# One decode step of attention and a gated MLP on one core: the query weights loaded in eight parts instead of one

## The chip, the cores and the metric

The kernel runs on one core of a Trainium2 chip. The metric is the device time of one execution in microseconds (us). Three executions of the kernel before took 2521.19, 2520.79 and 2520.80 us, median 2520.80 us.

## What is computed

One token `x` (1 x 512, bf16) goes through an attention block with a cache of 32 heads of 65,536 positions of 128 numbers, and through a gated MLP. A sigmoid gate mixes the two results.

```python
def _A_ref(x, k_cache, v_cache, wq, wo):          # wq: 512 x 4096, wo: 4096 x 512
    q = (x @ wq).reshape(B, Sq, H, Dh).transpose(0, 2, 1, 3)      # H = 32, Dh = 128
    scores = jnp.einsum("bhqd,bhkd->bhqk", q, k_cache) * (Dh ** -0.5)
    p = softmax(scores, axis=-1)
    o = jnp.einsum("bhqk,bhkd->bhqd", p, v_cache)
    return o.transpose(0, 2, 1, 3).reshape(B, Sq, H * Dh) @ wo

def _B_ref(x, w_gate, w_up, w_down):              # 512 x 1792, 512 x 1792, 1792 x 512
    return (silu(x @ w_gate) * (x @ w_up)) @ w_down

g = sigmoid((x * gate_w).sum(-1, keepdims=True))
out = g * A + (1 - g) * B
```

The keys and the values are 537 MB each. Every byte of them is needed once.

## The kernel before, in words

One large array in on-chip memory, `mem`, has 128 partitions with 184 slots of 512 bf16 numbers each. All weights and all parts of the cache are loaded into slots of it. SyncE issues nearly all loads from one queue, in the order in which its block is written (lines 201 to 244).

**The start.** `weights` (lines 207 to 209) issues one load of one weight array and lets it raise that array's semaphore by 16. Line 211 loads `wq` into the slots from `V0` on: 128 rows, one for each partition, of 16,384 bf16 numbers (32 KB), which makes 4,096 KB. Partition p gets rows 4p to 4p + 3 of `wq`, which lie one after the other in HBM. Lines 212 to 214 load `wg`, `wu` and `wd` in the same way (1,792 KB each), and line 217 the first half of head 0's keys in two loads of 4,096 KB. None of these seven issues waits for anything. Then SyncE waits for `s_q` (line 219) before it issues the second half of head 0's keys, because these go to the slots that `wq` has taken.

**The queries.** TensorE waits at line 436 until the semaphore of `wq` shows 16, makes all 32 heads' queries in 128 matmuls (line 439) and signals `s_q` (line 441). VectorE and TensorE bring the queries into the form that the scores need (lines 371 to 376 and 445). After that TensorE waits for `wg` and `wu` (line 467 holds the matmuls) and for `wd` (line 475).

**The heads.** For each head, VectorE transposes the keys in 16 pieces (line 331 for head 0, lines 399 and 406 for the others), and TensorE multiplies each piece by the query (line 455). A softmax follows (lines 272, 299, 301, 274), and VectorE rearranges its result (line 340). While the next head's scores are made, TensorE adds up the values (line 502). A cache half is one load of 8,192 KB. SyncE issues it (line 205) when the slots that it goes to have been read, which it learns from `ktdone` (keys transposed) or `pvdone` (values used).

**The end.** The values of the second part of the last head and `wo` arrive in smaller pieces (lines 235 to 244), the last products are made (lines 516, 531, 549), and ScalarE sends the result out (line 310).

Of the kernel before, what the change touches and what calls it, by code (L numbers as in the profile page):

```python
# [5 lines left out]
P = 128  # L6
KB = 512
# [13 lines left out]
def bass_gated_mix__mha_block_cached__swiglu_ffn__decode_kernel(  # L21
# [11 lines left out]
    out: bass.AP,  # L33
):
    _, H, S, Dh = A_k_cache.shape
    D = A_wq.shape[0]
    F = B_w_gate.shape[1]
    Dc = D // P
# [24 lines left out]
    with ExitStack() as ctx:  # L63
        def sb(name, shape, dt):
            return ctx.enter_context(nc.sbuf_tensor(name, shape, dt))
# [4 lines left out]
        def sem(name):  # L70
            return ctx.enter_context(nc.semaphore(name))
# [10 lines left out]
        mem = sb("mem", [P, MEM * KB], BF16)  # L82
# [24 lines left out]
        def at(kb, n):  # L107
            return mem[:, kb * KB:kb * KB + n]
# [9 lines left out]
        d = {n: sem("d_" + n) for n in names}  # L118
# [55 lines left out]
        w_dram = {  # L174
            "wq": A_wq.rearrange("(p c) n -> p (c n)", c=Dc),
            "wg": B_w_gate.rearrange("(p c) f -> p (c f)", c=Dc),
            "wu": B_w_up.rearrange("(p c) f -> p (c f)", c=Dc),
            "wd": B_w_down.rearrange("(p c) n -> p (c n)", c=FC),
            "wo": A_wo.rearrange("(p j) n -> p (j n)", p=P),
        }  # L180
        w31_dram = A_wo.rearrange("(h d) n -> h d n", d=Dh)[H - 1]
        WQ, WG, WU, WD, WO = V0, 0, 14, V0 + 64, 64
# [8 lines left out]
        def place(kind, h, z):  # L191
            if kind == "k":
                return (KA, V0)[z] if h == 0 else (KA, KZ)[z]
            return (VA, VZ)[z]

        def kv_dram(cache, h):
            return cache[0, h].rearrange("(b p r) d -> b p (r d)", b=2, p=P)
# [3 lines left out]
        @block.sync  # L201
        def _(sp):
            def load(kind, h, z):
                cache = A_k_cache if kind == "k" else A_v_cache
                sp.dma_start(at(place(kind, h, z), HR * Dh), kv_dram(cache, h)[z]).then_inc(d[kind + "az"[z]], 16)

            def weights(n, kb):
                src = w_dram[n]
                sp.dma_start(at(kb, src.shape[1]), src).then_inc(d[n], 16)  # L209

            weights("wq", WQ)
            weights("wg", WG)
            weights("wu", WU)
            weights("wd", WD)
            half = HR // 2 * Dh
            for n in range(2):
                sp.dma_start(at(KA + 32 * n, half), kv_dram(A_k_cache, 0)[0][:, n * half:n * half + half]).then_inc(  # L217
                    (d["ka0"], d["ka"])[n], 16)
            sp.wait_ge(s_q, 1)
            load("k", 0, 1)  # L220
            for h in range(1, H):
                sp.wait_ge(ktdone, 2 * NP * h - 3 if h > 1 else NP)
                load("k", h, 0)
                if h == 1:
                    sp.wait_ge(ktdone, 2 * NP - 3)
                    sp.wait_ge(s_b, 1)
                else:
                    sp.wait_ge(pvdone, 4 * h - 1)
                load("v", h - 1, 0)
                sp.wait_ge(ktdone, 2 * NP * h + NP // 2)  # L230
                load("k", h, 1)
                sp.wait_ge(pvdone, 4 * h + 1)
                load("v", h - 1, 1)
            sp.wait_ge(ktdone, 2 * NP * H - NP)
            weights("wo", WO)
            src = A_v_cache[0, H - 1].rearrange("(b p r) d -> b p (r d)", b=2, p=P)
            need = {0: (ktdone, 2 * NP * H - 3), 1: (ktdone, 2 * NP * H), 2: (pvdone, 4 * H - 1)}
            for n, (kb, r0, nr) in enumerate(tail):
                if n in need:
                    sp.wait_ge(*need[n])  # L240
                b, o = divmod(r0, HR)
                sp.dma_start(at(kb, nr * Dh), src[b][:, o * Dh:(o + nr) * Dh]).then_inc(dt_[n], 16)  # L242
            sp.wait_ge(pvdone, 4 * H)
            sp.dma_start(at(WO31, D), w31_dram).then_inc(d["w31"], 16)
# [183 lines left out]
        def _(pe):  # L428
# [4 lines left out]
                last = nc.tensor.matmul(psM[:, c:c + 1], xv[:, c, :], ones[0:1, 0:1], start=True, stop=True)  # L433
            last.then_inc(s_xT, 1)
            pe.wait_ge(s_xTb, 1)
            pe.wait_ge(d["wq"], 16)
            for h in range(H):
                for c in range(Dc):
                    last = nc.tensor.matmul(psM[:, 128 + h:129 + h], wq_ap[:, c, h * Dh:(h + 1) * Dh],  # L439
# [47 lines left out]
            with nc.tensor.Fori(0, H) as i:  # L487
                n = i * (2 * NP)
# [90 lines left out]
```

## Time and profile before

| what | value |
|---|---|
| median of three executions | 2520.80 us |
| the profiled execution: its time | 2521.39 us |
| the profiled execution: span, first to last instruction | 2519.6 us |
| time outside the span | 1.8 us |
| read from HBM | 1087.77 MB, 432 GB/s over the span |
| mean granted clock of TensorE | 0.711 of full speed |
| `wq`: issue, and first matmul that uses it | 0.72 us, 13.62 us |

The profile is a page of sums over the span and a trace that can be asked for more. The page has the busy time of each engine, the span in 40 slices, the DMA queues, the chain of work that ended last, and the groups of instructions by line. The trace also has a record of each DMA packet: when it started, how long it took and how many bytes it moved. PE is TensorE, PEld its weight loads, DVE VectorE, ACT ScalarE, POOL GpSimd, and SPq is SyncE's queue. L439 is line 439. A time is counted from the start of the span unless it is a duration.

### The profile page before, as it was taken

To read this page: it belongs to the slowest core of one execution; us is meant where nothing else is said; L and a number is where in the kernel's file an instruction comes from. 1 tells how busy PE (TensorE), PEld (TensorE's weight loads), DVE (VectorE), ACT (ScalarE), POOL (GpSimd) and SP (SyncE) were. 2 spreads that over 40 slices of the span, in tenths; PEclk is the share of its full clock that TensorE was granted. 3 is DMA by queue.
4 is the path that set the end of the run, shared out by engine and by line. 5 is a ranking of instruction groups with operands and counts; after the bars stand their busy time and mean duration, and the time that the engine had idled before them with its cause. 6 is when DMAs were issued, how large, how long until landed. Compare 5 with 4: busy or idle time off the path is not lost.

```text
span 2519.6 us, 46355 instructions
## 1 busy us (share of the span) xinstructions
PE 1587.1 (63%) x21429; PEld 890.1 (35%) x21429; DVE 1397.7 (55%) x1629; ACT 65.6 (3%) x195; POOL 26.9 (1%) x83
## 2 busy tenths in 40 slices
PE   4556756667666576565675665765657656567667
PEld 3333333333333333333333333333333333333334
DVE  3764564554655645646446555466464564654652
ACT  0000000000000000000000000000000000000000
POOL 0000000000000000000000000000000000000000
PEclk8667767677676676676776766767667767677676
DMA  9999999999999999999999999999999999999999
GB/s 419 434 433 432 433 433 434 434 433 433 434 433 433 433 433 433 433 434 434 433 433 433 434 434 436 435 435 433 433 433 433 434 434 434 434 433 433 434 433 386
DMA packets 20332, 1088.00 MB, mean 432 GB/s; under 512 B 2266, under 2 KB 2396, under 8 KB 2780
## 3 DMA queue, kind: packets, MB, share of 16 engines
q1 hardware_dynamic: 20304, 1087.78, 99.9%
q8 instruction: 11, 0.18, 0.0%
q14 instruction: 5, 0.04, 0.0%
q10 hardware_dynamic: 12, 0.00, 0.0%
HBM read 1087.77 MB, written 0.00 MB: 432 GB/s over the span
## 4 chain that ended last, share of the span: by engine, by line
DMA 73%; DVE 14%; issue 11%; PE 1%; SPq 0%; DVEq 0%; ACT 0%
DMA mem<-in_A_k_cache_dram 71%; DVE kt L406 7%; DVE kt L399 6%; DMA mem<-in_A_v_cache_dram 2%; PE psO L502 1%; DVE kt L331 0%; DVE pb L340 0%; DVEq L404 0%; SPq L242 0%; SPq L209 0%; DVEq L397 0%; PE psS L455 0%; PE psZ L549 0%; SPq L217 0%; PE psW L516 0%
## 5 line engine op out<-in xcount | busy, mean ns | idle before, releaser
L455 PE MATMUL psS<-qcur,kt 128*128 128x4 bf16 x16384 | 516.4, 167 | 886.1 <-DVE kt L399 553.2
L502 PE MATMUL psO<-mem,pb 128*4 128x512 bf16 x3968 | 999.6, 417 | 17.0 <-DMA mem<-in_A_v_cache_dram 17.0
L399 DVE STREAM_TRANSPOSE kt<-mem 128x2048 uint32<-128x2048 uint32 x248 | 551.2, 2280 | 578.4 <-DMA mem<-in_A_k_cache_dram 577.4
L455 PEld LDWEIGHTS psS<-qcur,kt 128*128 128x128 bf16 x16384 | 473.8, 104 | 955.1 <-DVE kt L399 586.4
L406 DVE STREAM_TRANSPOSE kt<-mem 128x2048 uint32<-128x2048 uint32 x248 | 547.6, 2275 | 407.5 <-DMA mem<-in_A_k_cache_dram 407.5
L502 PEld LDWEIGHTS psO<-mem,pb 128*4 128x4 bf16 x3968 | 354.4, 91 | 618.7 <-issue 186.2
L340 DVE COPY pb<-pa 32x64 bf16<-32x64 bf16 x1024 | 233.7, 228 | 25.5 <-PE psO L502 10.7
L331 DVE STREAM_TRANSPOSE kt<-mem 128x2048 uint32<-128x2048 uint32 x16 | 35.4, 2278 | 17.0 <-DMA mem<-in_A_k_cache_dram 17.0
L345 DVE TENSOR_REDUCE sm<-psS 128x1 f32<-128x512 f32 x32 | 22.1, 691 | 35.5 <-PE psS L455 35.5
L295 ACT ACTIVATE oTn<-psT,gcol 128x1 bf16<-128x1 f32 x31 | 8.2, 263 | 1113.3 <-PE psT L482 1113.3
L272 POOL PARTITION_ALL_REDUCE sm<-sm x32 | 11.2, 351 | 2392.8 <-DVE sm L345 2392.8
L482 PEld LDWEIGHTS psT<-unit,orow 4*128 4x128 f32 x256 | 30.8, 186 | 14.9 <-issue 13.5
L482 PE MATMUL psT<-unit,orow 4*128 4x1 f32 x256 | 33.5, 248 | 0.8 <-ACT orow L293 0.8
L293 ACT ACTIVATE orow<-psO,sm 4x512 f32<-4x512 f32 x31 | 21.0, 677 | 446.0 <-issue 446.0
L299 ACT ACTIVATE sm<-sm 128x1 f32<-128x1 f32 x32 | 6.5, 203 | 831.0 <-POOL sm L272 831.0
L301 ACT ACTIVATE pa<-psS,sm 128x512 bf16<-128x512 f32 x32 | 22.0, 687 | 1.0
L516 PE MATMUL psW<-pb,mem 128*128 128x1 bf16 x512 | 14.4, 165 | 5.6 <-DMA mem<-in_A_v_cache_dram 4.4
L516 PEld LDWEIGHTS psW<-pb,mem 128*128 128x128 bf16 x512 | 14.0, 102 | 6.8 <-issue 5.1
L274 POOL PARTITION_ALL_REDUCE sm<-sm x32 | 12.3, 384 | 36.4 <-ACT pa L301 36.4
L439 PE MATMUL psM<-xTb,mem 128*128 128x1 bf16 x128 | 3.5, 165 | 11.2 <-DMA mem<-in_A_wq_dram 11.2
L467 PE MATMUL psM<-xTb,mem 128*128 128x1 bf16 x112 | 6.9, 198 | 5.2 <-DMA mem<-in_B_w_up_dram 5.2
L531 PE MATMUL psY<-mem,oR 128*1 128x512 bf16 x32 | 9.7, 477 | 0.3 <-DVE oR L420 0.3
(62 smaller groups left out, 57.8 us busy)
## 6 DMA issues: line engine op xcount, KB each, us to landing
mem<-in_A_v_cache_dram SPq DMA_DIRECT2D x3, 4096.0 KB, 28.5
mem<-in_A_k_cache_dram SPq DMA_DIRECT2D x2, 4096.0 KB, 39.2
mem<-in_A_wq_dram SPq DMA_DIRECT2D x1, 4096.0 KB, 12.8
mem<-in_A_wo_dram SPq DMA_DIRECT2D x1, 4096.0 KB, 34.5
mem<-in_A_v_cache_dram SPq DMA_DIRECT2D x1, 2048.0 KB, 33.0
mem<-in_B_w_gate_dram SPq DMA_DIRECT2D x1, 1792.0 KB, 16.6
mem<-in_B_w_up_dram SPq DMA_DIRECT2D x1, 1792.0 KB, 21.7
mem<-in_B_w_down_dram SPq DMA_DIRECT2D x1, 1792.0 KB, 25.5
```

Source lines behind the costliest of these rows:

```text
L274: nc.gpsimd.partition_all_reduce(Lt, rsum, P, RADD).then_inc(s_L, 1)
L293: nc.scalar.mul(orow[0:4, :], psO[0:4, :], Li[0:4, :]).then_inc(s_or, 1)
L301: nc.scalar.activation(pa[:], psS[:], ACT.Exp, bias=nbias, scale=SCALE, accum_out=rsum).then_inc(expdone, 1)
L331: nc.vector.transpose(kt[:, i % 2, :].rearrange("p (j r t) -> p r j t", j=2, t=32), src.rearrange("p (r j t) -> p r j t", j=2, t=32)).then ...
L340: last = nc.vector.tensor_copy(dst, sr)
L345: nc.vector.reduce_max(mxs, psS[:], AX_X).then_inc(s_mx, 1)
L399: nc.vector.transpose(kt[:, c % 2, :].rearrange("p (j r t) -> p r j t", j=2, t=32), src.rearrange("p (r j t) -> p r j t", j=2, t=32)).then ...
L406: nc.vector.transpose(kt[:, c % 2, :].rearrange("p (j r t) -> p r j t", j=2, t=32), src.rearrange("p (r j t) -> p r j t", j=2, t=32)).then ...
L455: last = nc.tensor.matmul(psS[:, col + 4 * r:col + 4 * r + 4], ktb[c % 2][:, je // 2, r, :, je % 2], qcur[:, je, :], start=(je == 0), stop ...
L482: last = nc.tensor.matmul(psT[:, 0:1], orow[0:4, i * Dh:(i + 1) * Dh], unit[0:4, i:i + 1], start=(i == 0), stop=(i == 3))
L502: last = nc.tensor.matmul(psO[0:4, :], pb[:, 256 * z + r:256 * z + r + 4], vt[:, r * Dh:(r + 4) * Dh], start=(z == 0 and part == 0 and m = ...
L516: last = nc.tensor.matmul(psW[:, 0:1], vt[:, r * Dh:(r + 1) * Dh], pb[:, col:col + 1], start=(col == 0), stop=(col == R - 1))
```

## The change

The load of `wq` becomes eight loads. Load r takes partitions r, r + 8, r + 16 and so on up to r + 120, which are 16 partitions, and the 16 rows of 32 KB in HBM that belong to them. All eight raise the same semaphore, each by 16, and TensorE waits for 128 in place of 16. What lands in which place of `mem` is the same as before.

```diff
-            weights("wq", WQ)
+            for r in range(8):
+                sp.dma_start(mem[r:P:8, WQ * KB:WQ * KB + Dc * H * Dh],
+                             w_dram["wq"].rearrange("(g r) n -> r g n", r=8)[r]).then_inc(d["wq"], 16)
             weights("wg", WG)
...
             pe.wait_ge(s_xTb, 1)
-            pe.wait_ge(d["wq"], 16)
+            pe.wait_ge(d["wq"], 128)
```

## The prediction

> **What bounds the kernel now.** I read the page's top first, for the engines and the data moved.
>
> ```profile
> span 2519.6 us, 46355 instructions
> ...
> DMA  9999999999999999999999999999999999999999
> GB/s 419 434 433 432 433 433 434 434 433 433 434 433 433 433 433 433 433 434 434 433 433 433 434 434 436 435 435 433 433 433 433 434 434 434 434 433 433 434 433 386
> DMA packets 20332, 1088.00 MB, mean 432 GB/s; under 512 B 2266, under 2 KB 2396, under 8 KB 2780
> ## 3 DMA queue, kind: packets, MB, share of 16 engines
> q1 hardware_dynamic: 20304, 1087.78, 99.9%
> ```
>
> All 40 slices show the 16 DMA engines at 90% or more, and 38 of them move 432 to 436 GB/s. SyncE's queue q1 keeps the engines busy 99.9% of the span. No compute engine is above 63%. So the kernel is one stream of bytes, and its time is the stream's length plus a start and a tail.
>
> The packet records give the pace. A row of 32 KB takes an engine 1.213 us in the median and one of 64 KB 2.422 us, and the next row starts at most 0.03 us after the one before has ended. That is 27.0 GB/s for one engine, 432 for 16. The page's load groups sum to 141 loads on q1, and 20304 / 141 = 144 packets: 128 rows and 16 packets of 4 bytes that raise the semaphore, one for each engine. So each engine gets 8 rows of every load.
>
> Does the stream have room in which a delay would vanish? Page part 6 and the waits of SyncE's queue answer that.
>
> ```profile
> mem<-in_A_k_cache_dram SPq DMA_DIRECT2D x63, 29.7
> mem<-in_A_v_cache_dram SPq DMA_DIRECT2D x62, 26.1
> ```
>
> A cache half is 8.39 MB, which takes 19.4 us at 433 GB/s. From issue to landing it takes 29.7 us (keys) and 26.1 us (values). So when a load is issued there are still 10.3 or 6.7 us of other loads ahead of it. SyncE waits long for TensorE (1312.2 us in all) to free the slots, but the engines never run out. What delays the stream at the start is therefore not made up later.
>
> Last, the chain of waits and the timeline of SyncE's queue at both ends.
>
> ```profile
> 0.72 0.38 SPq L209 DMA_DIRECT2D mem<-in_A_wq_dram  x1
> 1.16 0.42 SPq L209 DMA_DIRECT2D mem<-in_B_w_gate_dram  x1
> 1.63 0.45 SPq L209 DMA_DIRECT2D mem<-in_B_w_up_dram  x1
> 2.12 0.53 SPq L209 DMA_DIRECT2D mem<-in_B_w_down_dram  x1
> 2.69 1.04 SPq L217 DMA_DIRECT2D mem<-in_A_k_cache_dram  x2
> 17.20 0.33 SPq L205 DMA_DIRECT2D mem<-in_A_k_cache_dram  x1
> ```
>
> ```profile
> 2480.15 36.12 DMA mem<-in_A_v_cache_dram
> 2516.27 0.05 issue
> 2516.32 0.39 PE psW L516 x8
> ```
>
> Columns are start and duration. The last loads land at 2516.3, and 3.3 us of work follow. At the start, SyncE has issued 18.1 MB by 3.7 us, 42 us of stream. The windows of 0.1 us show the first bytes at 1.7 us, 1.0 us after the issue of `wq`.
>
> **The change, part by part.**
>
> *Seven more issues on SyncE.* From row to row the issues stand 0.44, 0.47, 0.49 and 0.57 us apart, so seven add 2.6 to 4.0 us, some 3.4. `wg`, `wu`, `wd` and the first keys are issued that much later; the last of these at about 6.6 instead of 3.2 us. `wq`'s own bytes (8 x 1.213 = 9.7 us) cover that until 11.4 us. Each of the eight loads brings every engine 1.2 us of work and costs 0.5 us to issue, so the queue grows from the start. Cost: nothing. Were an issue to take over 1.2 us, the stream would have gaps.
>
> *The first bytes.* A shorter first load could start sooner, by at most the 1.0 us between issue and first packet, or not at all. The trace has no load of 16 rows; the nearest row is `wq`'s own. I take nothing.
>
> *Seven more sets of semaphore packets.* Each engine gets 7 more packets of 9 ns (their record): 0.06 us. Rounded, 0.1.
>
> *The wait for 128 in place of 16.* It passes when the last of the eight loads has landed; nothing else is queued on TensorE that could run in between, and VectorE and SyncE wait for `s_q` either way. When `wq` lands is uncritical: the slots of `wq` are wanted at line 219, issued at 17.2 us, while the bytes ahead of it last until 1.7 + 42 = 44 us. That is 26 us of cover. The next stop, `wu` at 23.5 us and the keys at 37.4 us, follows the stream itself.
>
> *Where the rows go.* This is the term that decides. In the load of 128 partitions each engine has eight partitions to itself. In a load of every eighth partition each engine has one row. The trace cannot say whether 27.0 GB/s is the pace of an engine or of the place that it writes to. If partitions are written through 16 groups of eight, each at that pace, and the partitions r, r + 8, ... fall on only half of the groups, then two engines share each group and each goes at half its pace. Order within the load doesn't matter: the 16 partitions are the same. Loads 0 to 3 would use one half of the groups and 4 to 7 the other, always with two engines in each. From below the price is nothing (groups and engines don't meet). From above it is `wq`'s stream once more: 8 x 1.213 = 9.7 us. I take 9.7, since all packet rows of one size show one and the same pace (1.213 to 1.225 us for 90% of the 32 KB rows), which looks like a fixed door rather than shared memory bandwidth, and a door that is full with one engine has nothing left for a second.
>
> [...]
>
> *HBM's side.* The eight loads read rows 256 KB apart (8 x 32 KB). The cache halves have 64 KB rows, so engines four rows apart read 256 KB apart too, at 433 GB/s. Cost: nothing.
>
> **Sum.** The stream after `wq` shifts by 9.7 + 0.1 = 9.8 us, and the end with it. On the profiled execution, 2521.39 (span 2519.6 and 1.8 around it), that is 2531.2. It lies 0.6 above the median 2520.8, so the forecast is 2530.6 us, +0.39%.
>
> **The rivals.**
>
> *A, not slower: a group takes two engines at full pace,* or rows are dealt so that engines don't meet. For it: an engine's own limit explains the constant packets as well. Against it: the fixed pace named above. Time: 2520.8 + 0.1 = 2520.9, at best 2519.9 with an earlier first byte. It decides if a pair reaches together over 1.32 times one engine's pace: 19.4 / 1.32 - 9.7 = 5.0 us, the 0.2% that a measurement can tell from no change.
>
> *B, the two of a pair drift apart.* If one engine of a pair is served first, it finishes its rows of loads 0 to 3 at full pace and moves to the other groups while its partner has the first to itself: 4 + 4 + 4 row times in place of 16. The loss is 4 x 1.213 = 4.9 us: 2525.7. For it: engines do drift, the semaphore packets of `wq` spread over 1.05 us. Against: that spread is less than one row.
>
> *C, each load pays a start.* An engine's first packet stands about 1.88 us before its second (in the earliest record) where later ones are 1.21 apart, 0.66 more. Seven times that is 4.6 us: 2525.5. Against it: in the trace the first packet of `wg` starts 6 ns after the first semaphore packet of `wq`; loads in the queue follow without a gap.
>
> That the change doesn't do what it says is no rival: it is eight plain loads.
>
> **How the numbers follow.** Forecast 0.66 (own range 2528.5 to 2532.5), A 0.17, B 0.10, C 0.05, something dearer 0.02. The predicted time is the forecast's. The range takes in the price's lower bound, nothing, and goes up to what two engines losing another fifth to each other would give, 2532.5: 2520.8 to 2532.5. Half of A lies about its low end. Faster by over 0.2% (below 2515.8) would need more than the 1.7 us that stand before the first byte: 0.01. Within 0.2%: A with C and half of B, less that: 0.17 + 0.05 + 0.05 - 0.01 = 0.26. Slower: 0.73.
>
> **What the changed profile would show.** Right: from 3 to 13 us some 216 GB/s where before had 402; rows of `wq` at some 2.4 us; line 439 starting at 23.4 in place of 13.6 us; the load of line 219 issued at 27 us; the page's first slice at (63 x 419 - 9.7 x 433) / 63 = 352 GB/s, the other 39 as before; q1 with 20304 - 144 + 8 x 32 = 20416 packets; the tail's 3.3 us unchanged. Wrong: line 439 near 13.6 us (A), near 18.5 (B, C), or a first slice of 419. If `wq` lands late and the end doesn't move, the stream had room that I read as none.

## The result, and the profile after

The changed kernel takes 2531.4 us (median of 6 executions, 2531.27 to 2531.56) against 2520.8 us before (6 executions, 2520.66 to 2521.19). The ratio is 1.0041, with a 95% interval of 1.0031 to 1.0051. It is 10.6 us slower; 9.8 us were forecast. The profiled execution took 2531.47 us with a span of 2529.6 us, 10.0 us more than the span before.

The page of the changed kernel, the same rows as before:

```profile
span 2529.6 us, 46362 instructions
...
GB/s 350 428 437 432 433 436 431 433 431 437 432 432 434 433 433 432 438 431 432 434 432 432 434 438 431 432 434 432 432 434 438 431 432 433 433 432 433 438 432 385
...
q1 hardware_dynamic: 20416, 1087.78, 99.9%
```

The first slice of 63 us has fallen from 419 to 350 GB/s. That is 69 x 63 us = 4.3 MB that weren't moved there, 10 us at 433 GB/s: the whole loss. The other slices stand about 433 as before. The engines are still busy 99.9% of the span, so the busy share hides the loss: in the first 20 us they are busy at half pace (210 GB/s from 3 to 13 us, where the kernel before has 402). The packets on q1 are the 20416 that eight loads in place of one make, 112 more: 7 x 16 packets that raise the semaphore, one for each engine and load. So all 16 engines take part in each of the eight loads. In the packet records, too, the 16 rows of a load start within 1.0 us of each other and then run side by side.

The timeline at the start, with start and duration in the first two columns:

```profile
0.72 5.25 SPq L212 DMA_DIRECT2D mem<-in_A_wq_dram  x8
...
6.01 0.58 SPq L209 DMA_DIRECT2D mem<-in_B_w_gate_dram  x1
...
7.58 0.91 SPq L219 DMA_DIRECT2D mem<-in_A_k_cache_dram  x2
...
23.74 3.55 PE L441 MATMUL psM<-xTb,mem 128*128 128x1 bf16 x128 [21.36 <-DMA mem<-in_A_wq_dram]
27.32 0.33 SPq L205 DMA_DIRECT2D mem<-in_A_k_cache_dram  x1
```

In the kernel before, the same matmuls were:

```profile
13.62 3.55 PE L439 MATMUL psM<-xTb,mem 128*128 128x1 bf16 x128 [11.23 <-DMA mem<-in_A_wq_dram]
```

Line 439 of before is now 441. It starts at 23.74 us in place of 13.62. In the packet records a row of `wq` takes 2.54 us in the median where it took 1.213, and the last row ends 20.7 us after the first has started, not 11.4.

The chain of waits at the end:

```profile
2489.74 36.52 DMA mem<-in_A_v_cache_dram
2526.27 0.05 issue
2526.31 0.39 PE psW L518 x8
```

The last load lands at 2526.27 us, 10.0 later than before, and 3.3 us of work follow as before. The 10 us lost in the first 24 us are carried through the whole stream; nothing is won back or added.

### The profile page after: what moved, and what is told of

Same layout as the page of the kernel before. It is cut to its first block, busy times and chain, and to the rows that moved or that the text cites. A ratio compares the mean times of both kernels' runs of the same rounds, so it can differ in the third digit from the quotient of the medians.

```text
span 2529.6 us, 46362 instructions
## 1 busy us (share of the span) xinstructions
PE 1588.2 (63%) x21429; PEld 890.2 (35%) x21429; DVE 1397.7 (55%) x1629; ACT 65.6 (3%) x195; POOL 26.9 (1%) x83
## 3 DMA queue, kind: packets, MB, share of 16 engines
q1 hardware_dynamic: 20416, 1087.78, 99.9%
## 4 chain that ended last, share of the span: by engine, by line
DMA 73%; DVE 14%; issue 11%; PE 1%; SPq 0%; DVEq 0%; ACT 0%
DMA mem<-in_A_k_cache_dram 71%; DVE kt L408 7%; DVE kt L401 6%; DMA mem<-in_A_v_cache_dram 2%; PE psO L504 1%; DVE kt L333 0%; SPq L212 0%; DVE pb L342 0%; DVEq L406 0%; SPq L244 0%; SPq L209 0%; DVEq L399 0%; PE psS L457 0%; PE psZ L551 0%; SPq L219 0%
## 5 line engine op out<-in xcount | busy, mean ns | idle before, releaser
L274 POOL PARTITION_ALL_REDUCE sm<-sm x32 | 11.2, 351 | 2403.5 <-DVE sm L347 2403.5
L441 PE MATMUL psM<-xTb,mem 128*128 128x1 bf16 x128 | 3.6, 165 | 21.4 <-DMA mem<-in_A_wq_dram 21.4
```

## The experiments

My theory: partitions are written through groups, and a load that reaches only some of the groups goes slower in proportion. How many groups there are, and which partitions share one, I assumed; no run shows it, and the counts of groups in what I expected rest on that assumption. What the runs show is the pace of the rows. Rivals: eight loads cost more than one whatever they hold; the late queries cost the time; the rows' distance in HBM does. Each experiment is an edit of the kernel before. Where a diff shows `wq` in several loads, TensorE waits for 16 for each of them; that line is left out of the diffs. The kernel before, run beside them on the same chip, had medians of 2521.06 us (the first four), 2520.89 (the next four) and 2520.91 (the last four).

### Eight loads, but by columns

```diff
-            weights("wq", WQ)
+            for r in range(8):
+                sp.dma_start(at(WQ + 4 * r, 4 * KB), w_dram["wq"][:, 4 * KB * r:4 * KB * (r + 1)]).then_inc(d["wq"], 16)
```

> The load of wq in eight loads by columns: each takes all 128 partitions and 4 KB of each row. Theory (two engines share a group of partitions): every engine has its own eight partitions again, so nothing is shared: within 1 us of before, 2520 to 2522 us, and line 439 starts within 1 us of 13.6 us. Rival (the price is that of eight loads in place of one: issues, semaphore packets, a start for each): 2531 us, as with the change.

Measured: 2521.34 us, ratio 1.0001 (0.9991 to 1.0011). In the profiled execution, which was 2.2 us above this median, `wq`'s first matmul starts at 14.55 us:

```profile
14.55 3.55 PE L440 MATMUL psM<-xTb,mem 128*128 128x1 bf16 x128 [12.17 <-DMA mem<-in_A_wq_dram]
```

Eight loads by themselves cost no time that can be told from nothing, though with 1,024 rows of 4 KB in place of 128 of 32 KB. The number of loads is not the price.

### Eight loads of 16 neighbours

```diff
-            weights("wq", WQ)
+            for r in range(8):
+                sp.dma_start(mem[16 * r:16 * r + 16, WQ * KB:WQ * KB + Dc * H * Dh],
+                             w_dram["wq"][16 * r:16 * r + 16, :]).then_inc(d["wq"], 16)
```

> Eight loads of 16 neighbouring partitions each, 0 to 15, 16 to 31 and so on; the number of loads, rows and bytes is that of the change. Theory: 16 neighbours lie in 4 groups, so four engines share each, and a row of 32 KB takes 4 x 1.213 = 4.85 us or a little more; wq takes 38.8 in place of 9.7 us: 2520.8 + 29 = 2550 us, up to 2552. Rival (eight loads cost 10 us wherever the rows lie): 2531 us. Rival (neighbours are what an engine likes): 2521 us.

Measured: 2547.41 us, +26.4, ratio 1.0104 (1.0087 to 1.0121). A row takes 4.61 us, 3.8 times 1.213.

```profile
39.53 3.55 PE L441 MATMUL psM<-xTb,mem 128*128 128x1 bf16 x128 [37.15 <-DMA mem<-in_A_wq_dram]
```

Loads, rows and bytes are those of the change, and the loss is 2.5 times as large. Which partitions a load holds decides. The size is a little under the 29 us expected: the rows take 4.61 instead of 4.85 us, and the first ones about 3.5.

### Two loads of 64 neighbours, and two of the even and odd partitions

```diff
-            weights("wq", WQ)
+            for r in range(2):
+                sp.dma_start(mem[64 * r:64 * r + 64, WQ * KB:WQ * KB + Dc * H * Dh],
+                             w_dram["wq"][64 * r:64 * r + 64, :]).then_inc(d["wq"], 16)
```

> Two loads, partitions 0 to 63 and 64 to 127. Theory: 64 partitions lie in 8 groups, two engines on each, as with the change: 2520.8 + 9.7 to 10.6 = 2530.5 to 2531.4 us with two loads only. Rival (a price for each added load): one load more, 10.6 / 7 = 1.5 us, 2522.3 us.

The other kernel has, in place of these lines:

```diff
+                sp.dma_start(mem[r:P:2, WQ * KB:WQ * KB + Dc * H * Dh],
+                             w_dram["wq"].rearrange("(g r) n -> r g n", r=2)[r]).then_inc(d["wq"], 16)
```

> [...] Theory as I have it, with rows dealt to the engines in runs (four rows for each engine, partitions 8e to 8e + 6): engines e and e + 4 are in the same group at the same time: 2530.5 to 2531.4 us, rows of some 2.5 us. Rival (what counts is only how many groups a load reaches, since the rows are dealt so that each engine has its own group): 2521 us, rows of 1.21 us.

Measured: the two halves take 2531.5 us, ratio 1.0041 (1.0027 to 1.0056), with rows of 2.56 us. The even and odd partitions take 2521.12 us, ratio 1.0001 (0.9991 to 1.001), with rows of 1.213 us. The timelines, first of the halves, then of the even and odd ones:

```profile
23.59 3.55 PE L441 MATMUL psM<-xTb,mem 128*128 128x1 bf16 x128 [21.21 <-DMA mem<-in_A_wq_dram]
```

```profile
13.94 3.55 PE L441 MATMUL psM<-xTb,mem 128*128 128x1 bf16 x128 [11.42 <-DMA mem<-in_A_wq_dram]
```

Two loads are enough for the whole loss, and two are enough for none. For the even and odd partitions my theory as stated missed (it had rows of some 2.5 us) and its rival's time held. Both kernels have 64 partitions in a load, so in these two it counts which partitions a load holds, and not how many. Why is not shown, since the trace does not record which engine took which row.

### Seven loads of partitions seven apart

```diff
-            weights("wq", WQ)
+            for r in range(7):
+                sp.dma_start(mem[r:112:7, WQ * KB:WQ * KB + Dc * H * Dh],
+                             w_dram["wq"][0:112].rearrange("(g r) n -> r g n", r=7)[r]).then_inc(d["wq"], 16)
+            sp.dma_start(mem[112:128, WQ * KB:WQ * KB + Dc * H * Dh], w_dram["wq"][112:128]).then_inc(d["wq"], 16)
```

> Seven loads of 16 partitions seven apart (r, r + 7, ... r + 105; r from 0 to 6), then one of the 16 partitions 112 to 127. Loads, rows and bytes are those of the change; only the spacing differs. [...] A count of row times with fair shares gives 12 in place of 8 (unshared) and 16 (eight apart): 14.6 us for wq, 4.9 us more than before, 2525.7 us (2525 to 2527). Rival (16 rows in a load cost the same wherever they lie): 2531.4 us.

Measured: 2530.48 us, +9.6, ratio 1.0037 (1.0023 to 1.0052). A miss: twice the expected loss, and near the rival's number.

```profile
22.82 3.55 PE L442 MATMUL psM<-xTb,mem 128*128 128x1 bf16 x128 [20.29 <-DMA mem<-in_A_wq_dram]
```

The packet records, taken 16 at a time in the order of their starts, show more. In the second, third and seventh load the median row takes 2.15, 2.24 and 2.19 us, in the sixth 1.84, in the fourth and fifth 1.66 and 1.64. In the last load, 16 neighbours, rows take 3.1 to 4.5 us. So the rival, one price wherever the rows lie, falls too. My count of row times rests on the assumption of which partitions share a group, which no run shows. It let rows that share with no other run at 1.213 us, and of the 112 rows in the seven loads none took less than 1.37 us. Why is not shown. The rows of a load start over 0.7 to 1.4 us, so for part of the time some engines are already in the next load.

### `wq` in one load, but later

```diff
-            weights("wq", WQ)
             weights("wg", WG)
             weights("wu", WU)
             weights("wd", WD)
+            weights("wq", WQ)
```

> wq in one load of 128 partitions as before, but issued after wd, so that the queries are made some 13 us later while the stream has the same bytes at the same pace. Theory (only the stream's length counts, there are 26 us of cover for the queries): 2520.8 us, within 1 us. Rival (the change costs its time because the queries come 10 us late): over 2531 us.

Measured: 2521.07 us, ratio 1.000 (0.9991 to 1.001).

```profile
27.33 3.55 PE L439 MATMUL psM<-xTb,mem 128*128 128x1 bf16 x128 [24.95 <-DMA mem<-in_A_wq_dram]
```

The queries come at 27.33 us, later than the changed kernel's 23.74, and it costs nothing. The late `wq` is a sign of the loss and not its cause.

### The same split at the end, on `wo`

```diff
-            weights("wo", WO)
+            for r in range(8):
+                sp.dma_start(mem[r:P:8, WO * KB:WO * KB + 32 * D],
+                             w_dram["wo"].rearrange("(g r) n -> r g n", r=8)[r]).then_inc(d["wo"], 16)
...
-            pe.wait_ge(d["wo"], 16)
+            pe.wait_ge(d["wo"], 128)
```

> wq as before; wo, which has the same shape and is loaded near the end, in eight loads of every eighth partition. Theory (any place in the stream costs the same, since it has no room anywhere): 2520.8 + 9.7 to 10.6 = 2530.5 to 2531.4 us. Rival (the price comes from the start, from cold queues or the first rows): 2521 us. Rival (near the end the stream has room, since SyncE waits for TensorE there): between 2521 and 2528 us.

Measured: 2532.13 us, +11.2, ratio 1.0044 (1.0027 to 1.0061), 0.7 us above the upper end expected. Two windows of this kernel, with the bandwidth in the last column:

```profile
2440.00:2480.00 40.00, 28.62 (x342) 15.23 (x341) 22.10 (x25) 1.24 (x4) 0.73 (x2) 0.74 1.03 351
2480.00:2490.00 10.00, 6.08 (x32) 2.75 (x29) 4.59 (x21) 0.94 (x2) 0.00 (x0) 0.88 0.90 279
```

The same windows of the kernel before:

```profile
2440.00:2480.00 40.00, 29.02 (x346) 15.45 (x345) 22.10 (x25) 1.24 (x4) 0.73 (x2) 0.74 0.99 428
2480.00:2490.00 10.00, 7.67 (x152) 5.50 (x149) 4.97 (x23) 0.94 (x2) 0.00 (x0) 0.76 1.01 436
```

The price is the same, a little more, some 2,470 us after the start. It does not belong to the start, and the stream has no room near its end either.

### Half of the columns in eight loads, half in one

```diff
-            weights("wq", WQ)
+            half_q = Dc * H * Dh // 2
+            for r in range(8):
+                sp.dma_start(mem[r:P:8, WQ * KB:WQ * KB + half_q],
+                             w_dram["wq"][:, 0:half_q].rearrange("(g r) n -> r g n", r=8)[r]).then_inc(d["wq"], 16)
+            sp.dma_start(at(WQ + 16, half_q), w_dram["wq"][:, half_q:2 * half_q]).then_inc(d["wq"], 16)
```

> Half of the columns of wq (16 KB of each row) in eight loads of every eighth partition, the other half in one load of 128 partitions. Nine loads in all. Theory: half the bytes at half the pace: 2520.8 + 4.9 to 5.3 = 2525.7 to 2526.1 us. Rival (a price for each load, 10.6 / 7 = 1.5 us): 2520.8 + 8 x 1.5 = 2532.9 us.

Measured: 2525.88 us, +5.0, ratio 1.0019 (1.001 to 1.0029). Half the bytes, half the loss, with one load more.

```profile
17.94 3.56 PE L443 MATMUL psM<-xTb,mem 128*128 128x1 bf16 x128 [15.57 <-DMA mem<-in_A_wq_dram]
```

### Place against source

The first kernel writes to every eighth partition but reads neighbouring rows of HBM; the second does the reverse.

```diff
-            weights("wq", WQ)
+            for r in range(8):
+                sp.dma_start(mem[r:P:8, WQ * KB:WQ * KB + Dc * H * Dh],
+                             w_dram["wq"][16 * r:16 * r + 16, :]).then_inc(d["wq"], 16)
```

> Eight loads into every eighth partition, as with the change, but load r reads the 16 neighbouring rows 16r to 16r + 15 of HBM; so the rows of wq lie in other partitions than the matmuls take them from, and the queries are of mixed-up weights. Theory (the place that is written to sets the pace): as with the change, 2531 to 2532 us, rows of 2.54 us. Rival (the rows' distance in HBM sets it): as with 16 neighbours, 2547 us, rows of 4.61 us.

```diff
-            weights("wq", WQ)
+            for r in range(8):
+                sp.dma_start(mem[16 * r:16 * r + 16, WQ * KB:WQ * KB + Dc * H * Dh],
+                             w_dram["wq"].rearrange("(g r) n -> r g n", r=8)[r]).then_inc(d["wq"], 16)
```

> Eight loads into 16 neighbouring partitions each, from every eighth row of HBM, 256 KB apart; again the rows lie in other partitions than the matmuls take them from. Theory (the place that is written to): 2547 us, rows of 4.61 us. Rival (the rows' distance in HBM): 2531 us, rows of 2.54 us.

Measured: 2531.17 us with rows of 2.54 us, and 2546.9 us with rows of 4.49 us. The ratios are 1.004 (1.0026 to 1.0055) and 1.0102 (1.0085 to 1.0119). Timelines, first the one that keeps the place, then the one that keeps the source:

```profile
23.41 3.55 PE L441 MATMUL psM<-xTb,mem 128*128 128x1 bf16 x128 [21.03 <-DMA mem<-in_A_wq_dram]
```

```profile
39.03 3.55 PE L441 MATMUL psM<-xTb,mem 128*128 128x1 bf16 x128 [36.64 <-DMA mem<-in_A_wq_dram]
```

Both follow the place that is written to. Where the rows come from in HBM is worth at most 0.12 us in a row of 4.6.

### Four loads: every fourth partition, and 32 neighbours

```diff
-            weights("wq", WQ)
+            for r in range(4):
+                sp.dma_start(mem[r:P:4, WQ * KB:WQ * KB + Dc * H * Dh],
+                             w_dram["wq"].rearrange("(g r) n -> r g n", r=4)[r]).then_inc(d["wq"], 16)
```

> Four loads of every fourth partition, 32 rows each, two for each engine. The theory of groups stands; open is how the rows are dealt. If engine e gets rows 2e and 2e + 1 (partitions 8e and 8e + 4), engines e and e + 4 meet: 2531 us, rows of 2.5 us. If the rows are dealt so that an engine's two rows lie 32 partitions apart, as the even and odd partitions at full pace suggest, no two meet: 2521 us, rows of 1.21 us.

The other kernel has `mem[32 * r:32 * r + 32, ...]` and rows `32 * r` to `32 * r + 31`, 32 rows in a load and so two for each of the 16 engines.

> [...] If an engine's two rows are neighbours, two engines share a group: 2531 us, rows of 2.5 us. If an engine's two rows lie 16 partitions apart, and all engines take their first row first, four share a group at a time: 2547 us, rows of 4.6 us.

Measured: every fourth partition 2521.21 us, ratio 1.0001 (0.9992 to 1.0011), rows of 1.218 us; 32 neighbours 2531.2 us, ratio 1.004 (1.0026 to 1.0055), rows of 2.55 us.

```profile
13.88 3.55 PE L441 MATMUL psM<-xTb,mem 128*128 128x1 bf16 x128 [11.50 <-DMA mem<-in_A_wq_dram]
```

```profile
23.39 3.56 PE L441 MATMUL psM<-xTb,mem 128*128 128x1 bf16 x128 [21.01 <-DMA mem<-in_A_wq_dram]
```

Every fourth partition is free, with rows of 1.218 us; every eighth pays, with rows of 2.54. Of the ways of dealing rows out that the two expectations name, the first answer fits an engine's two rows 32 partitions apart, and the second fits neighbours; neither of the two gives both answers, and no record shows how rows are dealt, so that stays open. All but the spacing of seven go at the whole pace, at about half of it or at about a quarter:

| load of `wq` | median row, us | times 1.213 us | against before, us |
|---|---|---|---|
| 128 partitions (before) | 1.213 | 1.00 | |
| even and odd / every fourth | 1.213 / 1.218 | 1.00 / 1.00 | +0.1 / +0.3 |
| every eighth (the change) | 2.54 | 2.09 | +10.6 |
| 32 / 64 neighbours | 2.55 / 2.56 | 2.10 / 2.11 | +10.3 / +10.4 |
| 16 neighbours | 4.61 | 3.80 | +26.4 |

## Why the prediction was right, and where it was not

**The stream bounds the kernel and has no room.** Right. +10.1 us at line 439, +10.0 us at the last landing. The same loss came from `wo` near the end, and half of it from half the columns.

**Where the rows go.** Right that the place that is written to decides: of the two kernels that move place and source apart, the one that keeps the place has rows of 2.54 us, the one that keeps the source 4.49. Rows take twice the time. The 16 groups of eight on which the price rests, and which partitions share one, are shown by no run; the runs show rows of 1.213 us, of 2.54 to 2.56 and of 4.61. The price was 9.7 us, 1.213 us for each of eight rows. Measured from first to last packet it is 20.7 - 11.4 = 9.3 us, with other parts. A pair of engines, in the prediction's terms, made 25.8 GB/s together (2 x 32 KB in 2.54 us) and not 27.0, so a row took 2.54 us and not 2.43, and seven rows lose 9.3 us in place of 8.5. The first row loses 0.2 us in place of 1.2, since it starts up slowly in both kernels (2.1 and 1.9 us to the second). These errors offset each other, so that 9.3 lies this close to 9.7 is in part luck. One row in the middle, the fifth, took 2.39 us. It is the first of loads 4 to 7, which the prediction sends to the other half of its groups; with always two engines in each it would be as long as the others, and why it is not was not tested. I had two engines meet because each has one row; in loads of 64 and 32 neighbours there are four and two rows for each engine, and a row takes 2.56 and 2.55 us all the same. How the rows are dealt is open.

**Seven more issues.** Free as forecast, but mis-sized: I had bounded them at 2.6 to 4.0 us, and `wg` is issued 4.85 us later (6.01 against 1.16). (The lower bound did not follow either: seven of the steps it names, 0.44 to 0.57, make 3.1 to 4.0.) An issue of 16 rows eight partitions apart holds SyncE's queue for 0.57 to 0.81 us, one of 128 rows held it for 0.38; with 16 neighbours it was 0.38 to 0.45, so the number of rows alone does not set it. The cover, `wq`'s own bytes, was still long enough. Ahead of the wait for `s_q` there were six issues before, not the seven that the description counts; there are thirteen now.

**The first bytes.** I bounded this between a gain of 1.0 us and nothing. It is a loss of 0.4 us. The windows show the first bytes in these stretches, before and after:

```profile
1.70:1.90 0.20, 0.00 (x0) 0.00 (x0) 0.17 (x2) 0.20 (x1) 0.00 (x0) 1.00 7.02 1802
```

```profile
2.10:2.30 0.20, 0.18 (x4) 0.19 (x4) 0.00 (x0) 0.20 (x1) 0.00 (x0) 1.00 7.31 1638
```

The first issue ends 0.23 us later, which is a part of it. The other kernels go the same way: where the first issue takes 0.38 us the first packet starts at 1.73 to 1.77 us, and where it takes 0.55 to 0.62, at 2.06 to 2.13. The 9.3 and the 0.4 make 9.7 us, by which the last packet of `wq` ends later. Two further bits are not in the sum. The first matmul comes 10.1 us later: between the last packet and it lie 0.46 us before and 0.89 now. That gap is 0.46 to 0.48 us also with the even and odd and with every fourth partition, and 0.9 to 1.5 in every kernel in which all loads of `wq` go below the full pace, so it goes with the pace; why is open. It delays the queries and not the stream. The last packet of the whole queue ends 10.0 us later (2526.13 against 2516.16), 0.3 more than that of `wq`, and where these 0.3 us lie was not found. So the profiled execution lost 10.1 us at the first matmul and 10.0 us at the end, where 9.8 were forecast.

**Semaphore packets, the wait for 128, HBM's side.** Right but for the packets' length: those of `wq`'s eight loads took 15 to 25 ns, 18 in the median, where that of the one load took 9, so they add some 0.13 us and not 0.06 to an engine. The load of line 219 is issued at 27.3 us, well before its bytes are due. The source plays no part that shows.

**The rivals.** A falls with the row of 2.54 us. C, a start for each load, falls with eight loads by columns and four of every fourth partition, both at +0.3 us. B, a pair drifting apart, falls with the records: rows after the first are all 2.4 to 2.6 us but for one at 2.19, where an engine that is served first would show rows of 1.2, and the 16 rows of a load never start more than 1.0 us apart.

**What the changed profile would show.** The window from 3 to 13 us has 210 GB/s where 216 were named, the first slice 350 where 352 were, and the tail 3.3 us.

## What to carry to other kernels

Before splitting a load, ask which partitions each part writes, not only how many: every second or every fourth partition was free here (rows of 1.213 and 1.218 us), every eighth and every run of 32 or 64 neighbours went at about half of the pace (2.54 to 2.56 us), and every run of 16 neighbours at about a quarter (4.61 us). A split by columns keeps all partitions in each load and cost nothing here (2521.34 against 2521.06 us). In this kernel, one full stream, the half-pace stretch showed in the GB/s of its slice (350 against 419) and not in the busy share (99.9% in both), and its whole loss, 10.0 us, arrived at the end.

## What the runs showed of the hardware that I had not expected

- With partitions seven apart, the median row of the second to the seventh load took 1.64 to 2.24 us, against 1.213, and it differed from load to load. None of the 112 rows of the first seven loads took less than 1.37 us. What slows them, and whether meetings between neighbouring loads have a part in it, was not tested.
- Sixteen rows of 32 KB took 2.54 us each with the change, which is 206 GB/s for 16 engines at once, and 4.61 and 4.49 us in the two kernels that write to 16 neighbours, 114 and 117 GB/s. For one engine alone 1.213 us are 27.0 GB/s. Counted by twos and fours that is 25.8 GB/s for two engines together and 28.4 to 29.2 for four, an estimate, since no record shows which engines share. In the two kernels that write to 16 neighbours the rows of a load start over 0.6 and 1.3 us, the larger spread with the shorter row, so 4.6 us is not shown to be the pace of one such load alone.
- In the four kernels that load `wq` whole at half pace, each engine's fifth row (the fifth 16 in the order of their starts) took 2.38 to 2.41 us where those around it took 2.54 to 2.56. In each it is the first row of the second half of `wq`: the first of load 4 of eight, of the third load of four, or of the second of two. With `wo` that row took 2.26 us in the median, and with half of the columns 1.11 where those around it took 1.26. With half of the columns it starts 4.3 us after the first row, with the change 9.7, so it goes with the order of the rows and not with the time. Why it is shorter no run tests.
